# Attention backward in one kernel: E transposes moved to the end of the step, fp32 X transposes cut into eight pieces, row factors by quarters

## The chip, the cores and the metric

One core of a Trainium2 chip runs the whole kernel. The metric is the device time of one execution in microseconds. A profiled execution gives the trace: when each instruction of each engine began and ended, and the transfers. The engines are TensorE (PE; its weight loads are listed apart as PEld), VectorE (DVE), ScalarE (ACT), GpSimd (POOL) and SyncE (SP), which issues most transfers.

## What is computed

The reference is a forward pass and its gradients (a VJP) for a block of attention gated by an MLP, at S = 2048 positions, D = 512, 32 heads of 16, F = 1792:

```python
def _A_ref(x, wqkv, wo):
...
    qkv = (lambda x, *d: x.transpose(*d))((x @ wqkv).reshape(B, S, 3, H, Dh), 2, 0, 3, 1, 4)
    q, k, v = qkv[0], qkv[1], qkv[2]
    scores = jnp.einsum("bhqd,bhkd->bhqk", q, k) * (Dh ** -0.5)
    p = _softmax(scores, axis=-1)
    o = jnp.einsum("bhqk,bhkd->bhqd", p, v)
    return (lambda x, *d: x.transpose(*d))(o, 0, 2, 1, 3).reshape(B, S, D) @ wo
...
x = A_x
xn = _layernorm(x, axis=-1)
s = _A_ref(xn, A_wqkv, A_wo)
g = _silu(_B_ref(xn, B_w1, B_b1, B_w2, B_b2))
return x + s * g
...
_out, _vjp = jax.vjp(_f, A_x, A_wqkv, A_wo, B_w1, B_b1, B_w2, B_b2)
_grads = _vjp(grad_out)
```

The change is in the attention: forward and backward of softmax(QK)V for all heads, done in one pass. For each pair of heads and each 512 queries the kernel needs E = exp(scores) and G = E times (dO V^T), both as [keys, queries], and both again transposed as [queries, keys] for the gradients of K and V.

## The kernel before, in words

The kernel has three stages: `Pre` (projections, MLP forward, the gate), `attention_core`, and `Grads` (the weight gradients and dx). The order of instructions on every engine is the order in which the program emits them; there is no scheduler. A semaphore wait stands wherever a buffer or a result is needed from another engine.

`attention_core` walks over 64 blocks (16 pairs of heads, 4 chunks of 512 queries), each of 16 steps (one per 128 keys): 1024 steps, g = 0 to 1023, and 20 more to drain. In step g, PE gets in this order:

- `emit_d` and `emit_s` (L1115, L1093): d(g) for two heads, and s(g+1), the scores of the next step. All four are 32-row matmuls of 512 columns. d has three PSUM buffers (`ps_d`), s has one, which is two banks wide (`ps_s`).
- `emit_T` (L1177): seven 128x128 bf16 transposes of E(g-1) into tT, of which there is one buffer (`ps_t`). The eighth tile goes by a DMA transpose (`ekd`).
- `emit_XT` (L1233): in step 2 of a block only (`FIN_AT`), four 128x128 fp32 transposes of xs, the sums X of the block before.
- `emit_x` (L1207, L1210, L1214): twelve matmuls of 256 columns that add to X; the last four ("gts matmuls") read G(g-1). X has one buffer.
- `emit_z` (L1291): four matmuls of 512 columns that add to Z, from step g-20's point of view, with E or G transposed as the moving side and row factors W1, W2 as weights. In steps 4 to 7 and 12 to 15 of a block Z reads W2 and G (`gk`), in steps 8 to 11 and 0 to 3 W1 and E (`ek`, `ekd`). Z has one buffer. There is no Z in the first 20 steps.

ScalarE computes the exponential ets(g+1) from s(g+1) (`emit_exp`, L1102) and then copies most of tT to `ek` (`emit_cT`, L1189). DVE makes the two products gts(g) = d(g) times ets(g) (`emit_mult`, L1132, "multiplies"), and in some steps, between them, the rest of tT: `VCOPY` says how many of the seven tiles DVE takes in which of the 16 steps (nine of them have one or two). DVE also copies X to xs behind the multiplies of step 0 (L1223), XT to xt in step 2 (L1245), takes a reciprocal of its 17th columns (L1255), and after steps 3 and 11 adds Z to acc (`emit_acc`, L1303, L1305) behind the multiplies. POOL computes the row factors and the outputs from xt in ten operations per block (`emit_fin`, L1256 to L1271), behind that reciprocal, and issues the loads of the next pair of heads (`late`), each behind a small copy that waits for a multiply (L1351). SP issues the DMA transposes of gts to gk every second step (L1148), and of two tiles of ets every eighth (L1158 to L1164).

In code, the order in a step before is:

```python
emit_d(g, 0); emit_s(g + 1, 0); emit_s(g + 1, 1); emit_d(g, 1)
emit_exp(g + 1)
emit_T(g - 1); emit_XT(g)
emit_x(g - 1, "e"); emit_x(g - 1, "l"); emit_x(g - 1, "g")
emit_z(g + ZOFF)
emit_mult(g); emit_xs(g - 1); emit_fin(g)
...
emit_acc(g + ZOFF)
emit_cT(g - 1, 0, 7 - VCOPY[(g - 1) % 16], nc.scalar.copy)
emit_dmat(g)
```

Of the kernel before, what the change touches and what calls it, by code (L numbers as in the profile page):

```python
# [1028 lines left out]
def attention_core(ctx, ctx_r, tc, k, grads, Oall, dQall, dKVT_out, ident_f32, ident_bf, npairs=16, nqc=4):  # L1029
# [75 lines left out]
    def emit_d(g, hj):  # L1105
        a = a_unit(g)
        if a is None:
            return
# [6 lines left out]
        nc.tensor.matmul(d[:], lhsT=op["KVT"][r:r + 32, kb * 128:(kb + 1) * 128], rhs=op["QDT"][r:r + 32, qc * 512:(qc + 1) * 512],  # L1115
                         start=True, stop=True, tile_position=(r, 0))


    VCOPY = (0, 0, 0, 0, 1, 1, 1, 2, 1, 2, 0, 0, 1, 1, 1, 0)

    def emit_mult(g):
        a = a_unit(g)
        if a is None:
            emit_cT(g - 1, 7 - VCOPY[(g - 1) % 16], 7, nc.vector.tensor_copy)
            return
        kb = a[1]
        if kb % 2 == 0:
            cur["gts"] = gtp.tile([128, 2, 2, 512], bf16, name="gts")
        gts = cur["gts"]
        st_gt[g] = gts  # L1130
        for hj in range(2):
            nc.vector.tensor_tensor(out=gts[:, kb % 2, hj, :].rearrange("k (b q) -> k b q", b=4),  # L1132
                                    in0=st_d.pop((g, hj))[:].rearrange("k (b q) -> k b q", b=4),
                                    in1=st_et[g][:, :, hj, kb % 4, :], op=ALU.mult)
# [33 lines left out]
    def emit_T(g):  # L1168
        a = a_unit(g)
        if a is None:  # L1170
            return
        kk = a[1] % 4
        et = st_et[g]
        t = ps_t.tile([128, 7, 128], bf16, name="tT")
        for i in range(7):
# [1 line left out]
            nc.tensor.transpose(t[:, i, :], et[:, b // 2, b % 2, kk, :], ident_bf[:])  # L1177
# [5 lines left out]
    def emit_cT(g, lo, hi, copy):  # L1183

        a = a_unit(g)
        if a is None or lo == hi:
            return
        j, kb = a
        copy(out=blk[j]["Ek"][kb // 4][:, kb % 4, lo:hi].rearrange("q i k -> q (i k)").bitcast(f32),  # L1189
             in_=st_T[g][:, lo:hi].rearrange("q i k -> q (i k)").bitcast(f32))  # L1190
# [26 lines left out]
    def emit_xs(g):  # L1217
# [5 lines left out]
        nc.vector.tensor_copy(out=xs[:], in_=blk[j].pop("X")[:])  # L1223
        blk[j]["xs"] = xs

    def emit_XT(g):
        j = g // 16 - 1
        if g % 16 != FIN_AT or not 0 <= j < NB:
            return
        xs = blk[j].pop("xs")  # L1230
        XT = ps_d.tile([128, 4, 128], f32, name="XT", tag="d")
        for qb in range(4):
            nc.tensor.transpose(XT[:, qb, :], xs[:, qb * 128:(qb + 1) * 128], ident_f32[:])  # L1233
        blk[j]["XT"] = XT

    def emit_fin(g):
        j = g // 16 - 1
        if g % 16 != FIN_AT or not 0 <= j < NB:
            return
        p, qc = blocks[j]  # L1240
        NQq = k.op0["NATQq"]
        NQd = k.op0["NATQd"]
        XT = blk[j].pop("XT")
        xt = xsp.tile([128, 4, 128], f32, name="xt", tag="xs")
        nc.vector.tensor_copy(out=xt[:], in_=XT[:])  # L1245
        xf = xt[:].rearrange("q b c -> q (b c)")
        XE = xf[:, 0:256].rearrange("q (b h c) -> q b h c", b=4, h=2)
        XG = xf[:, 256:512].rearrange("q (b h c) -> q b h c", b=4, h=2)
        W1, W2 = WT[j % 2]
        st0 = qc * 4  # L1250
        nqs = NQq[:, st0:st0 + 4, :, :]
        ndo = NQd[:, st0:st0 + 4, :, :]
        bc = lambda ap: ap.to_broadcast([128, 4, 2, 16])
        rL = finp.tile([128, 4, 2, 1], f32, name="rL")
        nc.vector.reciprocal(out=rL[:], in_=XG[:, :, :, 17:18])  # L1255
        nc.gpsimd.tensor_tensor(out=W2[:, :, :, 16:32], in0=nqs, in1=bc(rL[:]), op=ALU.mult)  # L1256
        ndl = finp.tile([128, 4, 2, 1], f32, name="ndl")
        nc.gpsimd.tensor_tensor(out=ndl[:], in0=XG[:, :, :, 0:1], in1=rL[:], op=ALU.mult)
        ndr = finp.tile([128, 4, 2, 1], f32, name="ndr")
        nc.gpsimd.tensor_tensor(out=ndr[:], in0=ndl[:], in1=rL[:], op=ALU.mult)  # L1260
        nc.gpsimd.tensor_tensor(out=W1[:, :, :, 0:16], in0=ndo, in1=bc(rL[:]), op=ALU.mult)
        nc.gpsimd.tensor_tensor(out=W1[:, :, :, 16:32], in0=nqs, in1=bc(ndr[:]), op=ALU.mult)
        Ov = Oall[:, st0:st0 + 4, p * 32:(p + 1) * 32].rearrange("q b (h c) -> q b h c", h=2)
        nc.gpsimd.tensor_tensor(out=Ov, in0=XE[:, :, :, 16:32], in1=bc(rL[:]), op=ALU.mult)
        t1 = finp.tile([128, 4, 2, 16], f32, name="t1")
        nc.gpsimd.tensor_tensor(out=t1[:], in0=XE[:, :, :, 0:16], in1=bc(ndl[:]), op=ALU.mult)
        nc.gpsimd.tensor_tensor(out=t1[:], in0=XG[:, :, :, 1:17], in1=t1[:], op=ALU.add)
        rL4 = finp.tile([128, 4, 2, 1], f32, name="rL4")
        nc.gpsimd.tensor_scalar(out=rL4[:], in0=rL[:], scalar1=0.25, scalar2=None, op0=ALU.mult)
        dQv = dQall[:, st0:st0 + 4, p * 32:(p + 1) * 32].rearrange("q b (h c) -> q b h c", h=2)  # L1270
        nc.gpsimd.tensor_tensor(out=dQv, in0=t1[:], in1=bc(rL4[:]), op=ALU.mult)  # L1271

    def emit_z(g):
        u = z_unit(g)
        if u is None:
# [4 lines left out]
        Z = blk[j]["Z"]  # L1280
        for par in range(2):
            kc = 2 * kp + par
            for hj in range(2):
# [7 lines left out]
                nc.tensor.matmul(Z[r:r + 32, :], lhsT=WT[j % 2][1 - part][:, qb, hj, :], rhs=mv,  # L1291
                                 start=(part == 0 and qb == 0), stop=(part == 1 and qb == 3), tile_position=(0, r))
# [184 lines left out]
```

## Time and profile before

| what | value |
|---|---|
| time, median of 3 runs | 2214.51 us (2211.53 to 2218.92) |
| the profiled execution, its own time | 2212.67 us |
| its span, first to last instruction | 2210.8 us |
| granted TensorE clock, mean | 0.997 |
| exponentials, L1102 | 1024, 1023 ns each |
| multiplies, L1132 | 2048, 683 ns each |
| reciprocals, L1255 | 64, 204 ns each |
| copies X to xs and XT to xt | 64 each, 680 ns each |

The profile gives busy times by engine, groups of instructions (line, engine, operation, what it writes and reads, how often, the busy time, the mean duration in ns of one, and the engine's idle time before them with what ended it), and timelines: start in us from the span's start, duration in us, engine, line, and how many instructions were merged into the row. A row with x7 and 0.55 is seven instructions whose first began at the start given and whose last ended 0.55 later. The engines work on several instructions in overlap, so a duration is longer than the distance between two starts.

### The profile page before, as it was taken

What the parts mean: (1) busy time and instruction counts of PE and PEld (TensorE: products, weight loads), DVE (VectorE), ACT (ScalarE), POOL (GpSimd) and SP (SyncE); (2) the same over time, 40 slices, a digit from 0 to 9 for tenths busy, and PEclk for the clock granted to TensorE, in tenths of its full rate; (3) what the DMA queues carried; (4) which work ended last, traced back from release to release, by engine and by line L of the source; (5) the groups of instructions that cost most, each with busy time, mean ns of one, the idle gap of its engine ahead of it and who ended that gap; (6) DMA issues with size and microseconds to landing.
All of it is one profiled execution on the core that took longest, in us unless ns stands there. A gap on an engine that the chain in (4) does not pass through costs nothing.

```text
span 2210.8 us, 74213 instructions
## 1 busy us (share of the span) xinstructions
PE 2154.0 (97%) x30690; PEld 1203.2 (54%) x30690; DVE 1911.7 (86%) x3638; ACT 1734.2 (78%) x2481; POOL 590.4 (27%) x1373
## 2 busy tenths in 40 slices
PE   6999999999999999999999999999999999999998
PEld 3444555555555555555555555555555555444444
DVE  6677899999999999999999999999999998797624
ACT  4664888888888888888888888888888887784214
POOL 4375213221222222221322122222222132510002
PEclk9999999999999999999999999999999999999999
DMA  7786999999999999999999999999999999999974
GB/s 232 244 277 200 200 199 192 202 198 194 204 205 195 204 196 197 201 197 202 200 196 203 199 195 198 206 194 204 197 197 206 197 210 211 300 259 235 244 200 156
DMA packets 1422066, 461.14 MB, mean 209 GB/s; under 512 B 1334622, under 2 KB 1405918, under 8 KB 1421728
## 3 DMA queue, kind: packets, MB, share of 16 engines
q1 hardware_dynamic: 1407424, 425.46, 101.4%
q0 software_dynamic: 12720, 29.37, 5.0%
q8 instruction: 240, 3.93, 0.8%
q10 hardware_dynamic: 1584, 1.57, 0.2%
q14 instruction: 98, 0.80, 0.1%
HBM read 62.79 MB, written 64.75 MB: 58 GB/s over the span
## 4 chain that ended last, share of the span: by engine, by line
PE 89%; DVE 4%; ACT 2%; issue 2%; DMA 2%; POOL 1%; SPq 1%; ACTq 0%; DVEq 0%; POOLq 0%
PE tT L1177 24%; PE d L1115 15%; PE X L1207 10%; PE Z L1291 10%; PE X L1210 5%; PE X L1214 5%; PE s L1093 3%; PE ps_dw L742 2%; PE ps_dy L912 2%; PE ps_h L352 2%; PE ps_dw L984 2%; PE ps_m L367 2%; PE ps_dh L878 2%; PE XT L1233 1%; PE ps_qkv L210 1%
## 5 line engine op out<-in xcount | busy, mean ns | idle before, releaser
L1132 DVE TENSOR_TENSOR gts<-d,ets 128x512 bf16<-128x512 f32 x2048 | 1361.6, 683 | 99.4 <-ACT ek L1189 20.5
L1102 ACT ACTIVATE ets<-s 128x1024 bf16<-128x1024 f32 x1024 | 1047.7, 1023 | 198.6 <-PE s L1093 95.5
L1177 PE MATMUL tT<-ident_bf,ets 128*128 128x128 bf16 x7168 | 568.1, 219 | 11.7 <-ACT ek L1189 1.7
L1177 PEld LDWEIGHTS <-ets 128*128 128x128 bf16 x7168 | 444.6, 97 | 237.6 <-issue 235.5
L1189 ACT COPY ek<-tT 128x448 f32<-128x448 f32 (+2 forms) x1024 | 502.2, 490 | 2.8 <-DVE ek L1189 2.1
L1115 PE MATMUL d<-QDT,KVT 32*128 32x512 bf16 x2048 | 459.1, 385 | 0.0
L1093 PE MATMUL s<-QDT,KVT 32*128 32x512 bf16 x2048 | 401.3, 380 | 3.7 <-ACT ets L1102 3.6
L1115 PEld LDWEIGHTS <-KVT 32*128 32x128 bf16 x2048 | 145.6, 91 | 323.3 <-issue 323.3
L1207 PE MATMUL X<-ets,NAT 128*32 128x256 bf16 x4096 | 300.4, 284 | 0.3 <-DVE xs L1223 0.3
L1210 PE MATMUL X<-ets,Lc 128*32 128x256 bf16 x4096 | 289.5, 273 | 0.0
L1214 PE MATMUL X<-gts,NAT 128*17 128x256 bf16 x4096 | 289.5, 273 | 0.0
L1351 POOL COPY tick<-gts 1x2 bf16<-1x2 bf16 x205 | 35.7, 174 | 612.3 <-DVE gts L1132 612.3
L1291 PE MATMUL Z<-gk,W 128*32 128x512 bf16 x2048 | 197.9, 379 | 1.0 <-DVE acc L1305 1.0
L1291 PE MATMUL Z<-ek,W 128*32 128x512 bf16 x1792 | 198.4, 379 | 0.0
L1207 PEld LDWEIGHTS <-NAT 128*32 128x32 bf16 x4096 | 106.0, 93 | 110.8 <-issue 11.3
L1256 POOL TENSOR_TENSOR W<-NATQq,rL 128x128 bf16<-128x128 bf16 x64 | 25.4, 396 | 526.1 <-DVE rL L1255 438.4
L1093 PEld LDWEIGHTS <-KVT 32*128 32x128 bf16 x2048 | 139.2, 91 | 12.8 <-issue 9.6
L1189 DVE COPY ek<-tT 128x64 f32<-128x64 f32 (+1 forms) x576 | 131.6, 229 | 0.7
L1291 PEld LDWEIGHTS <-W 128*32 128x32 bf16 x4096 | 109.8, 97 | 11.5 <-issue 1.5
L1210 PEld LDWEIGHTS <-Lc 128*32 128x32 bf16 x4096 | 107.8, 96 | 0.0
L1214 PEld LDWEIGHTS <-NAT 128*17 128x17 bf16 x4096 | 103.4, 92 | 3.0
L1291 PE MATMUL Z<-ekd,W 128*32 128x512 bf16 x256 | 97.0, 379 | 0.0
(246 smaller groups left out, 2318.7 us busy)
## 6 DMA issues: line engine op xcount, KB each, us to landing
gk<-gts SPq DMA_TRANSPOSE x512, 5.3
H1T_s<-h1r SPq DMA_DIRECT2D x28, 256.0 KB, 4.1
HGT_s<-hgT SPq DMA_DIRECT2D x8, 896.0 KB, 4.5
DH_s<-stg SPq DMA_DIRECT2D x12, 512.0 KB, 3.2
hch<-DH_s SPq DMA_DIRECT2D x12, 512.0 KB, 4.4
gp<-H1T_s SPq DMA_DIRECT2D x9, 512.0 KB, 7.6
out_dram<-ob_w POOLq DMA_DIRECT2D x36, 128.0 KB, 4.2
NAT_s<-NS SPq DMA_DIRECT2D x4, 1056.0 KB, 6.1
```

Source lines behind the costliest of these rows:

```text
L352: nc.tensor.matmul(ps[:], lhsT=w1_sb[:, ic, fc * 128:(fc + 1) * 128], rhs=yT[:, ic, g * 512:(g + 1) * 512], start=(ic == 0), stop=(ic == I ...
L367: nc.tensor.matmul(ps[:], lhsT=hgT[:, g % 2, fc, t4 * 128:(t4 + 1) * 128], rhs=w2_sb[:, fc, :], start=(fc == 0), stop=(fc == FC - 1))
L1093: nc.tensor.matmul(s[:, hj, :], lhsT=op["KVT"][r:r + 32, kb * 128:(kb + 1) * 128], rhs=op["QDT"][r:r + 32, qc * 512:(qc + 1) * 512], start ...
L1102: nc.scalar.activation(out=st_et[g][:, :, :, a[1] % 4, :].rearrange("k b h q -> k h b q"), in_=cur["s"][:].rearrange("k h (b q) -> k h b q ...
L1115: nc.tensor.matmul(d[:], lhsT=op["KVT"][r:r + 32, kb * 128:(kb + 1) * 128], rhs=op["QDT"][r:r + 32, qc * 512:(qc + 1) * 512], start=True, ...
L1132: nc.vector.tensor_tensor(out=gts[:, kb % 2, hj, :].rearrange("k (b q) -> k b q", b=4), in0=st_d.pop((g, hj))[:].rearrange("k (b q) -> k b ...
L1177: nc.tensor.transpose(t[:, i, :], et[:, b // 2, b % 2, kk, :], ident_bf[:])
L1189: copy(out=blk[j]["Ek"][kb // 4][:, kb % 4, lo:hi].rearrange("q i k -> q (i k)").bitcast(f32), in_=st_T[g][:, lo:hi].rearrange("q i k -> q ...
L1207: nc.tensor.matmul(X[r:r + 32, 0:256], lhsT=NATt[:, kb, hj, 1:33], rhs=ev, start=(kb == 0), stop=False, skip_group_check=True, tile_positi ...
L1210: nc.tensor.matmul(X[r:r + 32, 256:512], lhsT=Lc[:], rhs=ev, start=False, stop=False, skip_group_check=True, tile_position=(0, r))
L1214: nc.tensor.matmul(X[r:r + 17, 256:512], lhsT=NATt[:, kb, hj, 0:17], rhs=gv, start=False, stop=(kb == 15), skip_group_check=True, tile_pos ...
L1291: nc.tensor.matmul(Z[r:r + 32, :], lhsT=WT[j % 2][1 - part][:, qb, hj, :], rhs=mv, start=(part == 0 and qb == 0), stop=(part == 1 and qb = ...
```

## The change

Five things change, all in `attention_core`.

- The order of a step: Z now comes right after d and s, then X, and T at the end of the step.
- The copy of tT to ek is one copy of 448 fp32 columns on ScalarE in every step; `VCOPY` and DVE's share are gone.
- The four fp32 transposes of xs in step 2 become eight, one in each of steps 1 and 3 to 9 (`XT_AT`), each of 64 rows by 128 columns. Each stands right behind the seven transposes T of its step and writes the last 64 columns of the same tT buffer, which is now a whole bank. In the next step DVE copies it out first of all (`emit_xt`), into a part of xs that has been read already, or into xt0. The last block is done at once.
- The row factors (`fin_g`: reciprocal on DVE, five POOL operations) and the outputs (`fin_e`: five POOL operations) are computed for a quarter of the block behind each such copy: four pieces have a `fin_g`, the other four a `fin_e`.
- X's copy to xs and Z's addition to acc are emitted between the two multiplies of a step rather than behind them.

```diff
-    VCOPY = (0, 0, 0, 0, 1, 1, 1, 2, 1, 2, 0, 0, 1, 1, 1, 0)
...
             if hj == 0:
-                emit_cT(g - 1, 7 - VCOPY[(g - 1) % 16], 7, nc.vector.tensor_copy)
+                emit_xs(g - 1)
+                emit_acc(g + ZOFF)
...
-        t = ps_t.tile([128, 7, 128], bf16, name="tT")
+        t = ps_t.tile([128, 512], f32, name="tT")
+        tb = t[:].bitcast(bf16).rearrange("q (i k) -> q i k", k=128)
...
-            nc.tensor.transpose(t[:, i, :], et[:, b // 2, b % 2, kk, :], ident_bf[:])
+            nc.tensor.transpose(tb[:, i, :], et[:, b // 2, b % 2, kk, :], ident_bf[:])
...
+        nc.scalar.copy(out=blk[j]["Ek"][kb // 4][:, kb % 4].rearrange("q i k -> q (i k)").bitcast(f32), in_=st_T[g][:, 0:448])
...
+    XT_AT = {1: 0, 3: 1, 4: 2, 5: 3, 6: 4, 7: 5, 8: 6, 9: 7}
+
+    def piece(g):
+        j = g // 16 - 1
+        if not 0 <= j < NB - 1 or g % 16 not in XT_AT:
+            return None
+        return j, XT_AT[g % 16]
...
+    def transpose_piece(out, j, i):
+        q0 = (256, 0)[i // 4] + 128 * (i % 4 // 2)
+        h = i % 2
+        nc.tensor.transpose(out, blk[j]["xs"][64 * h:64 * h + 64, q0:q0 + 128], ident_f32[64 * h:64 * h + 64, 64 * h:64 * h + 64])
+
     def emit_XT(g):
...
+        pc = piece(g)
+        if pc is not None:
+            transpose_piece(st_T[g - 1][:, 448:512], *pc)
...
+    def emit_xt(g):
+        pc = piece(g)
+        if pc is None:
             return
...
+        j, i = pc
+        nc.vector.tensor_copy(out=slot_of(j, i), in_=st_T[g - 1][:, 448:512])
+        (fin_g if i < 4 else fin_e)(j, i % 4, i % 4 + 1)
...
+        emit_xt(g - 1)
         emit_d(g, 0)
         emit_s(g + 1, 0)
         emit_s(g + 1, 1)
         emit_d(g, 1)
         emit_exp(g + 1)
-        emit_T(g - 1)
-        emit_XT(g)
+        emit_z(g + ZOFF)
         emit_x(g - 1, "e")
         emit_x(g - 1, "l")
         emit_x(g - 1, "g")
-        emit_z(g + ZOFF)
+        st_T.pop(g - 2, None)
+        emit_T(g - 1)
+        emit_XT(g)
         emit_mult(g)
-        emit_xs(g - 1)
-        emit_fin(g)
...
-        emit_acc(g + ZOFF)
...
-        emit_cT(g - 1, 0, 7 - VCOPY[(g - 1) % 16], nc.scalar.copy)
-        st_T.pop(g - 1, None)
+        emit_cT(g - 1)
```

More of the change, by code (lines that the diff above doesn't have):

```diff
@@ L1135, in emit_mult @@
             if hj == 0:
-                emit_cT(g - 1, 7 - VCOPY[(g - 1) % 16], 7, nc.vector.tensor_copy)
+                emit_xs(g - 1)
+                emit_acc(g + ZOFF)
     def emit_dmat(g):
@@ L1181, in emit_T, with emit_cT @@
             blk[a[0]]["Ek"][a[1] // 4] = cur["ek"]
-    def emit_cT(g, lo, hi, copy):
+    def emit_cT(g):
         a = a_unit(g)
-        if a is None or lo == hi:
+        if a is None:
             return
         j, kb = a
-        copy(out=blk[j]["Ek"][kb // 4][:, kb % 4, lo:hi].rearrange("q i k -> q (i k)").bitcast(f32),
-             in_=st_T[g][:, lo:hi].rearrange("q i k -> q (i k)").bitcast(f32))
+        nc.scalar.copy(out=blk[j]["Ek"][kb // 4][:, kb % 4].rearrange("q i k -> q (i k)").bitcast(f32), in_=st_T[g][:, 0:448])
     def emit_x(g, part):
@@ L1224, in emit_xs @@
         blk[j]["xs"] = xs
-    def emit_XT(g):
-        j = g // 16 - 1
-        if g % 16 != FIN_AT or not 0 <= j < NB:
-            return
[L1230 to L1239, printed above, removed]
-        p, qc = blocks[j]
[L1241 to L1248, printed above, removed]
-        W1, W2 = WT[j % 2]
[L1250 to L1271, printed above, removed]
@@ new lines, in attention_core, with slot_of @@
+    XT_AT = {1: 0, 3: 1, 4: 2, 5: 3, 6: 4, 7: 5, 8: 6, 9: 7}
[4 more added lines that the diff above has]
+        return j, XT_AT[g % 16]
+    def slot_of(j, i):
+        if j == NB - 1:
+            return blk[j]["xs"][:, 64 * i:64 * i + 64]
+        if i == 0:
+            return xt0[:]
+        c = (192 + 64 * i) % 512
+        return blk[j]["xs"][:, c:c + 64]
+    def transpose_piece(out, j, i):
+        q0 = (256, 0)[i // 4] + 128 * (i % 4 // 2)
+        h = i % 2
+        nc.tensor.transpose(out, blk[j]["xs"][64 * h:64 * h + 64, q0:q0 + 128], ident_f32[64 * h:64 * h + 64, 64 * h:64 * h + 64])
@@ new lines, in emit_XT @@
+    def emit_XT(g):
+        pc = piece(g)
+        if pc is not None:
+            transpose_piece(st_T[g - 1][:, 448:512], *pc)
+        elif g == NSTEP + 1:
+            j = NB - 1
+            XT = ps_d.tile([128, 512], f32, name="XT", tag="d")
+            for i in range(4):
+                q0 = (256 + 128 * i) % 512
+                nc.tensor.transpose(XT[:, 128 * i:128 * i + 128], blk[j]["xs"][:, q0:q0 + 128], ident_f32[:])
+            nc.vector.tensor_copy(out=blk[j]["xs"][:], in_=XT[:])
+            fin_g(j, 0, 4)
+            fin_e(j, 0, 4)
@@ new lines, in fin_g @@
+    def fin_g(j, b0, b1):
+        XG, tt, bs, p, bc = fin_views(j, 0, b0, b1)
+        W1, W2 = WT[j % 2]
+        nqs = k.op0["NATQq"][:, tt, :, :]
+        ndo = k.op0["NATQd"][:, tt, :, :]
+        r, nl, nr = rL[:, bs], ndl[:, bs], ndr[:, bs]
+        nc.vector.reciprocal(out=r, in_=XG[:, :, :, 17:18])
+        nc.gpsimd.tensor_tensor(out=W2[:, bs, :, 16:32], in0=nqs, in1=bc(r), op=ALU.mult)
+        nc.gpsimd.tensor_tensor(out=nl, in0=XG[:, :, :, 0:1], in1=r, op=ALU.mult)
+        nc.gpsimd.tensor_tensor(out=nr, in0=nl, in1=r, op=ALU.mult)
+        nc.gpsimd.tensor_tensor(out=W1[:, bs, :, 0:16], in0=ndo, in1=bc(r), op=ALU.mult)
+        nc.gpsimd.tensor_tensor(out=W1[:, bs, :, 16:32], in0=nqs, in1=bc(nr), op=ALU.mult)
@@ new lines, in fin_e @@
+    def fin_e(j, b0, b1):
+        XE, tt, bs, p, bc = fin_views(j, 4, b0, b1)
+        XG = fin_views(j, 0, b0, b1)[0]
+        r, nl, r4 = rL[:, bs], ndl[:, bs], rL4[:, bs]
+        Ov = Oall[:, tt, p * 32:(p + 1) * 32].rearrange("q b (h c) -> q b h c", h=2)
+        nc.gpsimd.tensor_tensor(out=Ov, in0=XE[:, :, :, 16:32], in1=bc(r), op=ALU.mult)
+        t1 = XE[:, :, :, 0:16]
+        nc.gpsimd.tensor_tensor(out=t1, in0=t1, in1=bc(nl), op=ALU.mult)
+        nc.gpsimd.tensor_tensor(out=t1, in0=XG[:, :, :, 1:17], in1=t1, op=ALU.add)
+        nc.gpsimd.tensor_scalar(out=r4, in0=r, scalar1=0.25, scalar2=None, op0=ALU.mult)
+        dQv = dQall[:, tt, p * 32:(p + 1) * 32].rearrange("q b (h c) -> q b h c", h=2)
+        nc.gpsimd.tensor_tensor(out=dQv, in0=t1, in1=bc(r4), op=ALU.mult)
@@ L1312, in emit_acc @@
                 nc.gpsimd.dma_start(out=dv[:, kp, b, :], in_=ob[b * 64:(b + 1) * 64, :])
-    FIN_AT = 2
     ZOFF = -20
+    rL, ndl, ndr, rL4 = [finp.tile([128, 4, 2, 1], f32, name=n) for n in ("rL", "ndl", "ndr", "rL4")]
+    xt0 = finp.tile([128, 64], f32, name="xt0")
+    finp.tile([128, 128], mybir.dt.uint8, name="pad_to_256f")
     late = []
```

6 lines of the change are left out of this document (added).

## The prediction

> **What bounds the kernel now.** I read the page's busy shares, then the groups of instructions, then one line's instructions for the length of a step, and last the timeline of single steps, where the waits are. The shares:
>
> ```profile
> PE 2154.0 (97%) x30690; PEld 1203.2 (54%) x30690; DVE 1911.7 (86%) x3638; ACT 1734.2 (78%) x2481; POOL 590.4 (27%) x1373
> ```
>
> PE looks like the bound, but that share is an average and counts a matmul as busy while it drains. The groups the change touches, and the multiply's line:
>
> ```profile
> L1189 ACT COPY ek<-tT 128x448 f32<-128x448 f32 (+2 forms) x1024 | 502.2, 490 | 2.8 <-DVE ek L1189 2.1 <-PE tT L1177 0.6
> L1189 DVE COPY ek<-tT 128x64 f32<-128x64 f32 (+1 forms) x576 | 131.6, 229 | 0.7
> L1233 PE MATMUL XT<-ident_f,xs 128*128 128x128 f32 x256 | 38.9, 274 | 0.0
> ```
> ```profile
> L1132 DVE TENSOR_TENSOR gts<-d,ets x2048: 649/680/694, 222.7 to 1866.7; 128x512 bf16<-128x512 f32 x187
> ```
>
> From the first to the last multiply 1644.0 us pass, 1023 steps: 1.607 us a step, 25.70 us a block of 16. One step of it, in the timeline:
>
> ```profile
> 1001.21 1.02 ACT L1102 ACTIVATE ets<-s 128x1024 bf16<-128x1024 f32 x1
> ...
> 1002.13 0.53 ACT L1189 COPY ek<-tT 128x448 f32<-128x448 f32 x1
> ...
> 1002.28 0.38 PE L1115 MATMUL d<-QDT,KVT 32*128 32x512 bf16 x1
> 1002.29 0.39 PE L1093 MATMUL s<-QDT,KVT 32*128 32x512 bf16 x2
> ...
> 1002.61 0.47 PEld L1177 LDWEIGHTS <-ets 128*128 128x128 bf16 x7 [0.23 <-issue]
> ...
> 1002.71 0.55 PE L1177 MATMUL tT<-ident_bf,ets 128*128 128x128 bf16 x7
> 1002.81 1.02 ACT L1102 ACTIVATE ets<-s 128x1024 bf16<-128x1024 f32 x1 [0.15 <-PE s L1093]
> ...
> 1003.19 0.29 PE L1207 MATMUL X<-ets,NAT 128*32 128x256 bf16 x4
> ...
> 1003.53 0.39 PE L1291 MATMUL Z<-gk,W 128*32 128x512 bf16 x4
> ...
> 1003.85 0.38 PE L1115 MATMUL d<-QDT,KVT 32*128 32x512 bf16 x1
> ...
> 1003.88 0.39 PE L1093 MATMUL s<-QDT,KVT 32*128 32x512 bf16 x2
> ...
> 1003.98 0.48 ACT L1189 COPY ek<-tT 128x384 f32<-128x384 f32 x1 [0.15 <-DVE ek L1189]
> ...
> 1004.37 1.02 ACT L1102 ACTIVATE ets<-s 128x1024 bf16<-128x1024 f32 x1
> ```
>
> The reader is to see two waits that end together. The exponential of 1001.21 ends at 1002.23, and s starts at 1002.29; that of 1002.81 ends at 1003.83, s at 1003.88: s waits for its one buffer. The copy of 1002.13 ends at 1002.66 and the transposes T start at 1002.71, though their weights were being loaded from 1002.61: T waits for its one buffer. So the floor is a ring: exponential end to s 0.05, s to exponential 0.49 (1003.88 to 1004.37), exponential 1.02: **1.56**. PE alone would take d to T's load 0.32, T to X 0.48, X to Z 0.34, Z to d 0.32: 1.46. The rest of the 1.607 is the X transposes in one step of 16 and stalls behind acc and xs. The X transposes, a step without Z, and a transpose of 14 rows behind transposes of 128 (before the attention):
>
> ```profile
> 252.42 0.55 PE L1177 MATMUL tT<-ident_bf,ets 128*128 128x128 bf16 x7
> ...
> 252.81 0.61 PE L1233 MATMUL XT<-ident_f,xs 128*128 128x128 f32 x4
> ...
> 253.35 0.29 PE L1207 MATMUL X<-ets,NAT 128*32 128x256 bf16 x4
> ...
> 254.61 0.29 PE L1207 MATMUL X<-ets,NAT 128*32 128x256 bf16 x4
> ...
> 255.06 0.39 PE L1115 MATMUL d<-QDT,KVT 32*128 32x512 bf16 x1
> ```
> ```profile
> 26.94 0.38 PE L173 MATMUL tp_ps<-ident_bf,nat 128*128 128x128 bf16 x4
> ```
> ```profile
> 27.25 0.09 PEld L279 LDWEIGHTS <-b_bf 14*128 14x128 bf16 x1
> ```
>
> **The change, part by part.** D is the start of d in a step, us.
>
> *T to the end of the step.* T no longer waits: its buffer is copied out at about D+0.7 and wanted at D+1.0. But the floor of 1.56 does not contain T. New order on PE: d to Z 0.32 (as d to T); Z to X 0.22 (512 columns, by X's 0.11 for 256 with no change of tile shape between); X to T 0.45 (254.61 to 255.06); T to d 0.48 (as T to X): 1.47, as before. The ek copy now starts after T, so a second ring appears, over two steps: s to Z 0.32, to X 0.22, to T 0.45, T to its last result 0.55, to ScalarE 0.10 (s ends 1004.27, exponential 1004.37), copy 0.53 less 0.09 (the next exponential starts 0.09 before a copy ends: 1004.46 against 1004.37), exponential 1.02, to s 0.05: 3.15, or **1.57** a step. A plain step gains nothing.
>
> *The copy wholly on ScalarE.* DVE loses 131.6 us, ScalarE's copies go to 1024 x 0.53 = 543 us, 41 more. Neither is a sum on the path: ScalarE needs 0.93 + 0.44 = 1.37 a step. The cover is the 1.57; it is gone only where DVE falls behind (below).
>
> *Eight fp32 pieces.* Removed: the four of 128 columns in step 2, 0.54 from XT to X where T to X would take 0.48 less 0.39: 0.45 a block. Added, in eight steps of 63 blocks (the last block does it at once, as before): a 64-row, 64-column transpose between T and d. How soon it follows T, no row shows. Low end 0.056, by XT behind T (of seven starts 0.39 apart); high end 0.19, by the load of 14 rows behind 128-row transposes, which starts 0.15 after the last (26.94 + 0.38 - 0.22 = 27.10 to 27.25) plus 0.04, since an fp32 load lasts 140 ns against 97. I take 0.165: every row where the tile shape changes shows 0.09 to 0.10 beyond the stream (T to X 0.15 against 0.056), and this piece changes it. The Trainium skill, "TensorEngine Tiling (Array Packing)", Key Properties, says that a change of tiling mode drains TensorE; 128 rows to 64 is one. By it the low end is out; by the XT row alone a piece would cost 0.11 less. In the built changed kernel the piece shares T's buffer, the ek copy waits for the piece too, DVE's copy of the piece waits for the ek copy, and the next T waits for that. So in a piece step: T 0.34 to its last start, 0.165, piece 0.22 (273 ns less half its 107 stream), to ScalarE 0.10, copy 0.53, to DVE 0.05, copy of 64 columns 0.21, to T 0.05: **1.665**. PE alone: 1.47 + 0.165 = 1.635; the two-step ring (3.15 + 0.165)/2 = 1.66. Three limits at once; I take 1.66, between 1.60 (0.056: (3.15 + 0.056)/2) and 1.69 (0.19).
>
> The Trainium skill's "PSUM — Partial Sum Buffer", bank collisions, says that two engines must not read one bank at once; by it this wait cannot be dropped by the program. Here the copies of 1003.73 on DVE and 1003.98 on ScalarE do run in turn.
>
> *What queues behind the piece's copy.* It stands first in DVE's queue, so both multiplies wait: copy done at about D+0.95, four times a block a reciprocal behind it (203 ns, 0.035 after the copy), then the multiplies, whose starts are 0.60 apart (two in a row take 1.27) and of which the last lasts 0.68: end D+2.4. The gts matmuls of X want it at D+1.66+0.32+0.22+0.22 = D+2.42: no stall, nothing to spare. POOL's five row-factor operations a quarter (0.2 to 0.4 us each) fit in a step of 1.66, and Z wants a quarter 0.9 us after its reciprocal. SP's transposes and POOL's loads keep their places.
>
> *acc and xs between the two multiplies, Z first.* The second multiply then ends at D+0.49+0.60+0.60+0.68 = D+2.37, X wants it at D+1.57+0.76 = D+2.33, and 0.05 passes between: 0.09 in steps 1 and 12, about 0.15 in step 4, where DVE also comes late from the first piece: 0.34 a block. Before, the like stalls were in the 25.70.
>
> *The sum.* 8 x 1.57 + 8 x 1.66 + 0.34 = 26.18 against 25.70: +0.48 a block, x 63 = **+30 us**. The profiled execution took 2212.67 (span 2210.8 and 1.9 around it), 1.8 below the median of the runs, 2214.51; on that median 2245. With 1.60: 25.70, +0 us; with 1.69: +45 us.
>
> **Rivals.**
> 1. *The piece follows T as XT did.* Piece step 1.60, no change: 2215. For: the XT row. Against: the same row has no change of tile shape, all others do.
> 2. *The piece is hidden; faster.* PE has 0.10 spare a step (1.57 less 1.47). If the piece takes no more, and its copy leaves before T wants the buffer, 16 x 1.57 + 0.34 = 25.46, -0.24 x 63 = -15: 2200. It decides below a piece step of (25.70 - 12.56 - 0.34)/8 = 1.60. For: DVE loses 131.6 us, T's wait goes. Against: the copy chain.
> 3. *DVE becomes the bound.* If xt, reciprocal and multiplies end 0.1 late in four steps and the acc step doubles its stall, +0.5 a block, +32 on the forecast: 2277. For: DVE is over 90% busy in the attention and the margin is 0.02. Against: it loses 0.13 a step in 9 steps of 16.
>
> **How the numbers follow.** Forecast 0.62 (2225 to 2262); rival 1 0.09, rival 2 0.14, rival 3 0.15. A difference under 0.3%, 6.6 us, can't be told from none here. Faster is rival 2 with a part of rival 1: 0.15; same 0.08; slower 0.77. Range 2205 to 2282: rival 1 and the upper part of 2, to rival 3 with the high end of the piece.
>
> **What would show it.** Right: steps 3 to 9 of a block 1.64 to 1.68 apart, plain ones 1.56 to 1.58; T released by DVE's piece copy in piece steps; the piece 0.15 to 0.19 behind the last T; ek copies all 128x448. Wrong: a piece 0.06 behind T, s still 0.05 behind the exponential in piece steps, or plain steps under 1.55, which would mean a ring with less in it than I see.

## The result and the profile after

The changed kernel took 2273.01 us (median of 4, 2269.70 to 2273.93) against 2215.34 for the kernel before, measured beside it (median of 4): 1.027 times as long, with a 95% interval of 1.0253 to 1.0286. The forecast was 2245, with a range to 2282: the direction and the range held, the size was half of what came. The profiled execution took 2273.3 us, span 2271.2, mean clock 0.996 (before 2212.67, 2210.8 and 0.997).

The page of the kernel after, its shares and the groups of the copies and of the pieces:

```profile
PE 2218.8 (98%) x30891; PEld 1216.8 (54%) x30942; DVE 1893.0 (83%) x3692; ACT 1796.4 (79%) x2481; POOL 914.4 (40%) x3263
...
L1189 ACT COPY ek<-tT 128x448 f32<-128x448 f32 x1024 | 545.5, 533 | 188.4 <-PE tT L1244 149.2
...
L1265 DVE COPY xs<-tT 128x64 f32<-128x64 f32 x441 | 99.2, 225 | 75.7 <-ACT ek L1189 64.9
...
L1244 PE MATMUL tT<-ident_f,xs 64*128 64x64 f32 x504 | 136.9, 272 | 0.0
```

The view of the multiply's line (minimum, median, maximum in ns; start of the first and the last):

```profile
L1131 DVE TENSOR_TENSOR gts<-d,ets x2048: 670/681/693, 222.2 to 1924.8; 128x512 bf16<-128x512 f32 x187
```

First to last multiply is now 1702.6 us against 1644.0: +58.6, which is the whole of the difference. So the loss lies inside the 1024 steps and not in the stages around them. DVE is less busy than before (83% against 86%) and the multiplies are no slower. What is new in the groups is the idle time in front of ScalarE's copy: 149.2 us of it ended with a piece (L1244), and before it was 2.8 in all.

The timeline from step 4 of a block to step 6. Rows that show one step's wait are kept:

```profile
1026.07 0.39 PE L1115 MATMUL d<-QDT,KVT 32*128 32x512 bf16 x1
...
1026.08 0.38 PE L1115 MATMUL d<-QDT,KVT 32*128 32x512 bf16 x1
...
1026.74 0.23 DVE L1265 COPY xs<-tT 128x64 f32<-128x64 f32 x1
...
1027.00 0.17 DVE L1282 RECIPROCAL rL<-xs 128x2 f32<-128x2 f32 x1
...
1027.05 0.56 PE L1178 MATMUL tT<-ident_bf,ets 128*128 128x128 bf16 x7
1027.11 1.29 DVE L1131 TENSOR_TENSOR gts<-d,ets 128x512 bf16<-128x512 f32 x2
...
1027.55 0.27 PE L1244 MATMUL tT<-ident_f,xs 64*128 64x64 f32 x1
...
1027.75 0.39 PE L1115 MATMUL d<-QDT,KVT 32*128 32x512 bf16 x1
...
1027.85 0.37 PE L1115 MATMUL d<-QDT,KVT 32*128 32x512 bf16 x1
1027.86 0.53 ACT L1189 COPY ek<-tT 128x448 f32<-128x448 f32 x1 [0.23 <-PE tT L1244]
...
1028.15 0.40 PE L1320 MATMUL Z<-gk,W 128*32 128x512 bf16 x4
...
1028.82 0.56 PE L1178 MATMUL tT<-ident_bf,ets 128*128 128x128 bf16 x7
...
1029.31 0.27 PE L1244 MATMUL tT<-ident_f,xs 64*128 64x64 f32 x1
...
1029.51 0.38 PE L1115 MATMUL d<-QDT,KVT 32*128 32x512 bf16 x1
...
1029.52 0.39 PE L1115 MATMUL d<-QDT,KVT 32*128 32x512 bf16 x1
```

Three readings. First, the piece: T begins at 1027.05, the piece at 1027.55, d at 1027.75. A step without a piece has d 0.15 behind the last T; here the piece is 0.15 behind it and d 0.20 behind the piece. Second, the second d of a step: in the steps that begin at 1026.07 and 1029.51 it follows the first by 0.01, in the one at 1027.75 by 0.10. It writes one of three buffers, the one that the first multiply of the step before must leave. That multiply started at 1027.11, behind a copy and a reciprocal (1.04 after its step's d), and 0.69 later, at about 1027.8, the buffer is free. Third, what that delays: Z follows the second d by 0.30 to 0.31 in any case, so the step that begins at 1027.75 lasts 1.76 and the one before it 1.68.

Distances between the first d matmuls of neighbouring steps, worked out from the starts in the traces, in us. The rows are medians over the blocks; the last column is the sum of the means of all 16 steps:

| kernel | 0 | 1 | 2 | 3 | 4 | 5 | 6 | 7 | 8 | 9 | 10 | 11 | 12 | 13 to 15 | block |
|---|---|---|---|---|---|---|---|---|---|---|---|---|---|---|---|
| before | 1.56 | 1.63 | 1.99 | 1.48 | 1.67 | 1.56 | 1.55 | 1.57 | 1.55 | 1.54 | 1.59 | 1.53 | 1.64 | 1.55 to 1.56 | 25.69 |
| after | 1.55 | 1.94 | 1.48 | 1.93 | 1.68 | 1.76 | 1.68 | 1.76 | 1.68 | 1.68 | 1.48 | 1.61 | 1.56 | 1.55 | 26.63 |

26.63 less 25.69 is 0.94 a block; times 63 blocks, 59 us.

### The profile page after: what moved, and what is told of

Its sections match the earlier page's. It is cut to its first block, busy times and chain, and to the rows that moved or that the text cites. A ratio compares the mean times of both kernels' runs of the same rounds, so it can differ in the third digit from the quotient of the medians.

```text
span 2271.2 us, 76421 instructions
## 1 busy us (share of the span) xinstructions
PE 2218.8 (98%) x30891; PEld 1216.8 (54%) x30942; DVE 1893.0 (83%) x3692; ACT 1796.4 (79%) x2481; POOL 914.4 (40%) x3263
## 3 DMA queue, kind: packets, MB, share of 16 engines
q10 hardware_dynamic: 1584, 1.57, 0.2%
## 4 chain that ended last, share of the span: by engine, by line
PE 87%; DVE 4%; issue 3%; ACT 2%; POOL 2%; DMA 2%; SPq 1%; ACTq 0%; DVEq 0%; POOLq 0%
PE tT L1178 21%; PE d L1115 14%; PE Z L1320 14%; PE X L1213 5%; PE X L1206 5%; PE X L1209 5%; PE tT L1244 4%; PE s L1093 2%; PE ps_dy L912 2%; PE ps_dw L984 2%; PE ps_h L352 2%; PE ps_m L367 2%; PE ps_dw L742 2%; PE ps_dh L878 2%; PE ps_dwkv L830 1%
## 5 line engine op out<-in xcount | busy, mean ns | idle before, releaser
L1131 DVE TENSOR_TENSOR gts<-d,ets 128x512 bf16<-128x512 f32 x2048 | 1308.0, 683 | 66.3 <-issue 27.1
L1189 ACT COPY ek<-tT 128x448 f32<-128x448 f32 x1024 | 545.5, 533 | 188.4 <-PE tT L1244 149.2
L1178 PEld LDWEIGHTS <-ets 128*128 128x128 bf16 x7168 | 403.6, 98 | 207.7 <-issue 192.3
L1115 PE MATMUL d<-QDT,KVT 32*128 32x512 bf16 x2048 | 471.0, 383 | 0.1
L1213 PE MATMUL X<-gts,NAT 128*17 128x256 bf16 x4096 | 303.0, 273 | 0.1
L1283 POOL TENSOR_TENSOR W<-NATQq,rL 128x32 bf16<-128x32 bf16 (+1 forms) x253 | 60.8, 240 | 546.8 <-DVE rL L1282 484.2
L1115 PEld LDWEIGHTS <-KVT 32*128 32x128 bf16 x2048 | 139.9, 90 | 87.9 <-issue 0.2
L1265 DVE COPY xs<-tT 128x64 f32<-128x64 f32 x441 | 99.2, 225 | 75.7 <-ACT ek L1189 64.9
L1093 PEld LDWEIGHTS <-KVT 32*128 32x128 bf16 x2048 | 133.8, 90 | 16.2 <-issue 8.2
L1244 PE MATMUL tT<-ident_f,xs 64*128 64x64 f32 x504 | 136.9, 272 | 0.0
L1213 PEld LDWEIGHTS <-NAT 128*17 128x17 bf16 x4096 | 117.6, 91 | 16.8 <-issue 13.5
```

The costliest lines, as they stand in the source:

```text
L1093: nc.tensor.matmul(s[:, hj, :], lhsT=op["KVT"][r:r + 32, kb * 128:(kb + 1) * 128], rhs=op["QDT"][r:r + 32, qc * 512:(qc + 1) * 512], start ...
L1178: nc.tensor.transpose(tb[:, i, :], et[:, b // 2, b % 2, kk, :], ident_bf[:])
L1189: nc.scalar.copy(out=blk[j]["Ek"][kb // 4][:, kb % 4].rearrange("q i k -> q (i k)").bitcast(f32), in_=st_T[g][:, 0:448])
L1213: nc.tensor.matmul(X[r:r + 17, 256:512], lhsT=NATt[:, kb, hj, 0:17], rhs=gv, start=False, stop=(kb == 15), skip_group_check=True, tile_pos ...
L1244: nc.tensor.transpose(out, blk[j]["xs"][64 * h:64 * h + 64, q0:q0 + 128], ident_f32[64 * h:64 * h + 64, 64 * h:64 * h + 64])
L1265: nc.vector.tensor_copy(out=slot_of(j, i), in_=st_T[g - 1][:, 448:512])
```

## Experiments

After the result two explanations stood against each other for the piece steps. The expectations call them A, the pieces' own time on PE (the transpose and the change of tile shape on both sides of it), and B, the chain of copies that a piece lengthens (T, piece, ScalarE's copy, DVE's copy, next T). Each ratio below is against the kernel before, on the same chip. The runs were made in three batches on two chips, with the kernel before at 2213.49, 2215.15 and 2214.19 us, so a difference between runs of two batches is good to about 2 us.

### The new order without the pieces (order_only)

All of the change but the pieces and the quarters: the X transposes are four of 128x128 in step 2 again, behind T, and xt, reciprocal and row factors follow as before.

Against the changed kernel:

```diff
-        emit_xt(g - 1)
...
-        pc = piece(g)
-        if pc is not None:
-            transpose_piece(st_T[g - 1][:, 448:512], *pc)
...
+        if g % 16 != FIN_AT or not 0 <= j < NB:
+            return
+        XT = ps_d.tile([128, 4, 128], f32, name="XT", tag="d")
+        for qb in range(4):
+            nc.tensor.transpose(XT[:, qb, :], xs[:, qb * 128:(qb + 1) * 128], ident_f32[:])
...
+        emit_fin(g)
```

> The new order of the step, the whole copy of tT on ScalarE, xs and acc between the multiplies, but the X transposes whole in step 2 and the row factors at once, as before. Theory A (the eight pieces cost the time: each adds 0.20 us to PE in a step that has 0.07 to 0.13 us to spare): this kernel has none, its plain steps are 1.55 as in the changed kernel (median of steps 12 to 15), step 2 has 0.45 us more, so 16 x 1.55 + 0.45 + about 0.2 of stalls behind xs and acc = 25.45 a block against 25.70: about 15 us under the kernel before, 2200 (2190 to 2212). Theory C (the order or ScalarE's longer copy costs): 2240 to 2275.

Measured 2229.60, 1.0072 (1.0055 to 1.0089): 16 us slower than before, where a gain of about 15 was expected under A and 2240 or more under C: neither came. The plain steps are 1.551, so the estimate of those was right; the 0.48 a block by which it missed 25.45 is in one place. The timeline at steps 2 to 4 of a block:

```profile
1002.83 0.61 PE L1232 MATMUL XT<-ident_f,xs 128*128 128x128 f32 x4
...
1003.47 0.69 DVE L1244 COPY xt<-XT 128x512 f32<-128x512 f32 x1 [0.27 <-PE XT L1232]
...
1004.20 0.20 DVE L1254 RECIPROCAL rL<-xt 128x8 f32<-128x8 f32 x1
1004.32 0.65 DVE L1131 TENSOR_TENSOR gts<-d,ets 128x512 bf16<-128x512 f32 x1
...
1004.88 0.68 DVE L1302 COPY acc<-Z 128x512 f32<-128x512 f32 x1
...
1005.02 0.37 PE L1115 MATMUL d<-QDT,KVT 32*128 32x512 bf16 x1
1005.48 3.23 DVE L1131 TENSOR_TENSOR gts<-d,ets 128x512 bf16<-128x512 f32 x5
1005.61 0.40 PE L1290 MATMUL Z<-gk,W 128*32 128x512 bf16 x4 [0.23 <-DVE acc L1302]
```

The copy of XT (0.69) and the reciprocal stand ahead of step 3's multiplies, the acc copy between them. So acc comes out of Z's one buffer at 1005.56, Z of step 4 waits for it until 1005.61, and behind that the last multiply of step 3 is late for X. Step 4 lasts 2.08 against the 1.55 of a plain step: 0.53 x 63 = 33 us.

### The same, with the X transposes one step earlier, and with Z two steps later (order_xt_step1, order_z22)

Both take the collision out of order_only, in two ways. The first moves the X transposes to step 1, the second shifts Z and acc by two steps.

```diff
-    FIN_AT = 2
+    FIN_AT = 1
```
```diff
-    ZOFF = -20
+    ZOFF = -22
```

> The order-only kernel with the whole X transposes in step 1 instead of step 2. Theory D (its loss of 16 us against the kernel before is the 0.53 us by which step 4 is long: XT's copy and reciprocal on DVE in step 2 push the sum of Z into acc, in step 3, so late that Z in step 4 waits 0.28 and its gts matmuls another 0.17): with XT a step earlier DVE has step 2 to catch up, step 4 falls to 1.55 to 1.6, about 0.45 x 63 = 28 us under the order-only kernel and 12 under the kernel before: 2201 (2195 to 2212). Rival (the stall only moves to steps 1 to 3): 2220 to 2235.

> The order-only kernel with Z 22 steps behind instead of 20, so that acc falls in steps 5 and 13 and not right behind XT in step 2. Theory D: step 4's 0.53 goes, and step 6 takes no new stall, since DVE has steps 3 and 4 to catch up: about 30 us under the order-only kernel: 2199 (2193 to 2210). Rival (the new order needs these stalls whatever the place): 2220 to 2235.

Measured 2217.07, 1.0008 (0.9998 to 1.0019), and 2215.34, 1.0000 (0.9988 to 1.0013). The collision went in both: step 4 falls from 2.08 to 1.65 and to 1.63. Neither gains anything over the kernel before, which both expectations had asked for. With Z shifted, the sum of a block is 25.66, and before it is 25.69. So in the three arrangements tried the order is worth nothing at best: its plain step, 1.551, is the ring of s and the exponential (0.051 from the exponential's end to s, 0.477 to the next one, 1.024 for it), 0.01 less than before. Order and copy alone are not where the 58 us come from, and not a source of a gain either.

### A piece that nothing reads (dummy64)

order_only, and behind T in steps 1 and 3 to 9 one fp32 transpose of 64 rows of the identity, into the last 64 columns of tT's bank. Nothing reads these columns; what the kernel computes is unchanged. Against order_only:

```diff
+    def emit_dummy(g):
+        if g < 16 or g >= NSTEP or g % 16 not in (1, 3, 4, 5, 6, 7, 8, 9):
+            return
+        h = g % 2
+        nc.tensor.transpose(st_T[g - 1][:, 448:512], ident_f32[64 * h:64 * h + 64, :], ident_f32[64 * h:64 * h + 64, 64 * h:64 * h + 64])
...
+        emit_dummy(g)
         emit_XT(g)
```

> The order-only kernel with eight more 64-row fp32 transposes per block (of the identity), behind T in steps 1 and 3 to 9, into the last 64 columns of tT; nobody reads them, so the ek copy waits for them but DVE does nothing for them. Extra work, the outputs stay those of the reference. Theory A: PE alone then takes 1.68 in those steps against 1.55, +0.13 x 8 x 63 = +66 us on the order-only kernel, less what step 3 absorbs: +60 (50 to 68). Theory B (the chain ek copy, DVE's piece copy, next T, and the multiplies behind that copy, is what costs): +0 to +20.

Measured 2289.98, 1.0344 (1.0329 to 1.0360): 60.4 us over order_only, as A asked; B asked for under 20. Steps 3 and 5 to 9 last 1.683, the same as steps 4, 6, 8 and 9 of the changed kernel. Step 3 in the timeline, from d to the next d:

```profile
1030.79 0.38 PE L1115 MATMUL d<-QDT,KVT 32*128 32x512 bf16 x1
...
1031.77 0.56 PE L1178 MATMUL tT<-ident_bf,ets 128*128 128x128 bf16 x7
...
1032.27 0.27 PE L1276 MATMUL tT<-ident_f 64*128 64x64 f32 x1
...
1032.47 0.39 PE L1115 MATMUL d<-QDT,KVT 32*128 32x512 bf16 x1
```

The piece costs its time with no copy behind it, and no wait stands between T, the piece and d.

### The piece is also copied (dummy64_copied)

dummy64, and DVE copies the 64 columns first of all in the next step, into bytes that nothing uses. No reciprocal follows.

```diff
+        if 16 <= g - 1 < NSTEP and (g - 1) % 16 in (1, 3, 4, 5, 6, 7, 8, 9):
+            nc.vector.tensor_copy(out=xt0, in_=st_T[g - 2][:, 448:512])
```

> As the kernel before this one, and DVE copies each dummy piece first of all in the next step, as the changed kernel does, without reciprocal or row factors (the copy goes to unused bytes). Theory A: the ring T, piece, ek copy, piece copy, T is 0.346 + 0.150 + 0.308 + 0.533 + 0.032 + 0.225 + 0.090 = 1.684, the same as PE alone, and the first multiply ends at D+1.54, under 1.68: +0 to +8 us on the kernel without the copies. Theory B: +40 or more.

Measured 2292.46, 1.0355 (1.0340 to 1.0371): 2.5 us over dummy64; the intervals of the two ratios overlap, so that is hardly told from none. The copy moves the first multiply from 0.49 to 0.81 behind its step's first d, and that alone delays nothing: in piece steps 5 to 9 the distances are 1.683 again. Step 3 is longer by 0.19 and step 4 shorter by as much: XT holds one of the three d buffers there, and the second d of step 3 waits for the last multiply of step 2. The next T starts 0.09 behind the end of the copy, and 0.05 is what T takes behind a copy that it waits for: 0.04 to spare.

### A piece of T's own shape, ahead of T (dummy128_first)

order_only, and ahead of the seven transposes one fp32 transpose of 128x128 identity, written to columns that T then writes or that nothing reads. There is no change of tile shape between it and T, and T covers it from the copy.

```diff
+        emit_dummy(g + 1)
         for i in range(7):
...
+        nc.tensor.transpose(st_T[g - 1][:, 384:512], ident_f32[:], ident_f32[:])
```

> The order-only kernel with eight more 128x128 fp32 transposes per block ahead of T in the same steps (T overwrites half of what they write; nobody reads the rest). No tile shape changes between them and T. Theory A with the change of shape as the larger part of a piece's price: a transpose adds 0.11 us (the spacing of XT's four), of which 0.07 a step is spare: +0.04 x 8 x 63 = +20 us on the order-only kernel (10 to 30). If an fp32 transpose costs the same wherever it stands and whatever its shape: +60.

Measured 2271.07, 1.0260 (1.0242 to 1.0277): 41.5 over order_only, where 10 to 30 was expected. The last four matmuls of X to the first T are 0.378 apart against 0.216 without it, so it costs PE 0.162, not the 0.11 of four such transposes in a row:

```profile
1028.43 0.28 PE L1214 MATMUL X<-gts,NAT 128*17 128x256 bf16 x4
...
1028.65 0.33 PE L1276 MATMUL tT<-ident_f 128*128 128x128 f32 x1
...
1028.81 0.55 PE L1180 MATMUL tT<-ident_bf,ets 128*128 128x128 bf16 x7
```

T's seven starts take 0.011 less behind it, so a piece step is PE's 1.482 + 0.162 - 0.011, measured 1.634. The steps' means add up to 26.60 a block against 25.93 in order_only: 0.68 x 63 = 43. Twice the rows, and still 0.04 cheaper than 64 rows behind T. Why it costs more than in a row, where its neighbours are fp32 too, no run here shows.

### A piece of the shape of d, behind T (dummy32)

dummy64 with 32 rows and 32 columns: the tile shape of d, which comes next.

```diff
+        h = g % 4
+        nc.tensor.transpose(st_T[g - 1][:, 448:480], ident_f32[32 * h:32 * h + 32, :], ident_f32[32 * h:32 * h + 32, 32 * h:32 * h + 32])
```

> The order-only kernel with eight dummy pieces as in the 64-row run, but of 32 rows by 128 columns with 32 moving columns: the tile shape of the d and s matmuls that come next, so one change of shape stands between T and d, as without a piece. Nobody reads them; the outputs stay those of the reference. If PE's change of shape and the piece's stream are the price, PE alone falls from 1.68 to about 1.53 a step. What is left is the two-step ring, because the ek copy still waits for the piece: 0.974 (s to T) + 0.346 + 0.150 + 0.308 + 0.533 - 0.104 + 1.027 + 0.058 = 3.29, 1.645 a step, +0.09 x 8 x 63 = +47 us on the order-only kernel (40 to 52), 13 under the 64-row run. Rival (the ring through ScalarE doesn't count, PE alone does): +0 to +10 on the order-only kernel.

Measured 2265.60, 1.0228 (1.0208 to 1.0248): 36 over order_only, which ran on the other chip (35 by the two ratios), between the two expectations. The timeline of two steps:

```profile
1023.03 0.56 PE L1178 MATMUL tT<-ident_bf,ets 128*128 128x128 bf16 x7
...
1023.53 0.24 PE L1276 MATMUL tT<-ident_f 32*128 32x32 f32 x1
1023.53 0.38 PE L1115 MATMUL d<-QDT,KVT 32*128 32x512 bf16 x1
...
1023.81 0.53 ACT L1189 COPY ek<-tT 128x448 f32<-128x448 f32 x1 [0.62 <-PE tT L1276]
1024.23 1.03 ACT L1102 ACTIVATE ets<-s 128x1024 bf16<-128x1024 f32 x1
...
1025.08 0.38 PE L1115 MATMUL d<-QDT,KVT 32*128 32x512 bf16 x1
1025.32 0.39 PE L1093 MATMUL s<-QDT,KVT 32*128 32x512 bf16 x2
```

On PE this piece is nearly free: d follows it by 0.005, and T to d is 0.155 against 0.152 without it. The exception is step 6, where the piece lies on rows 64 to 95, those of the first d:

```profile
1026.80 0.24 PE L1276 MATMUL tT<-ident_f 32*128 32x32 f32 x1
1026.87 0.39 PE L1093 MATMUL s<-QDT,KVT 32*128 32x512 bf16 x2
1026.88 0.38 PE L1115 MATMUL d<-QDT,KVT 32*128 32x512 bf16 x2
```

There d comes 0.081 behind it, in all blocks (0.080 to 0.085). The 64-row piece delays d by 0.204 on either half of the rows, also on rows 0 to 63, which the two d do not use (steps 4, 6 and 8 of dummy64). So sharing rows is not what the 0.204 is, and the shape is.

ScalarE's copy, though, waits for the piece's last result: in the first timeline it starts 0.43 behind the start of the last T (1023.03 + 0.35 to 1023.81), without a piece 0.257. The exponential follows the copy, and s follows the exponential: at 1025.32 it is 0.24 behind its step's d. That is the two-step ring of the prediction. By the distances of order_only's trace (s to Z 0.324, to X 0.226, to the last X 0.218, to T 0.216, to the last T 0.346, to the copy 0.257, copy 0.533, less 0.091, exponential 1.023, to s 0.051) it takes 3.103 for two steps, 1.552 each; with 0.173 more, 1.638. Steps 8 and 9 together measure 3.270, 1.635 each. In steps 1, 3 and 4 other waits hide it, so 36 us rather than the 43 that 0.086 in all eight would give. A piece that took nothing from PE would thus still have lost 36 of the 60 us that the 64-row piece costs order_only.

### The reciprocal between the multiplies (late_recip)

The changed kernel, with the reciprocal and the row factors called between the two multiplies. The copy of the piece stays in front.

```diff
-        (fin_g if i < 4 else fin_e)(j, i % 4, i % 4 + 1)
...
+                emit_fin(g - 1)
                 emit_xs(g - 1)
```

> The changed kernel with the reciprocal and the row factors moved from the front of DVE's step to the place between the two multiplies; the copy of the piece stays first. Theory A (in steps 3, 5 and 7 the second d matmul waits for a d buffer that the first multiply of the step before frees late, because the reciprocal stands ahead of it): the first multiply starts at D+0.81 instead of D+1.01 to 1.04, the wait goes from steps 5 and 7 and shrinks by 0.2 in step 3: 0.07 + 0.07 + 0.2 = 0.34 a block, 21 us under the changed kernel: 2252 (2245 to 2260), if Z in steps 5 to 7 doesn't wait for a row factor that comes 0.6 later. Rival (that wait is harmless, the step is bound by the piece on PE): 2268 to 2275.

Measured 2258.99, 1.0202 (1.0186 to 1.0219): 14 us under the kernel after, where 21 was expected; the time is within the expected range. The timeline of steps 4 and 5:

```profile
1017.99 0.38 PE L1115 MATMUL d<-QDT,KVT 32*128 32x512 bf16 x1
...
1018.65 0.22 DVE L1267 COPY xs<-tT 128x64 f32<-128x64 f32 x1
1018.80 0.68 DVE L1132 TENSOR_TENSOR gts<-d,ets 128x512 bf16<-128x512 f32 x1
...
1019.39 0.15 DVE L1289 RECIPROCAL rL<-xs 128x2 f32<-128x2 f32 x1
...
1019.67 0.39 PE L1115 MATMUL d<-QDT,KVT 32*128 32x512 bf16 x1
...
1019.68 0.38 PE L1115 MATMUL d<-QDT,KVT 32*128 32x512 bf16 x1
```

The first multiply starts at 1018.80, 0.81 behind its step's first d where after it was 1.04; its buffer is free at 1019.48, and the second d of step 5 no longer waits (1019.68). Steps 5 and 7 go from 1.757 to 1.684, step 3 from 1.931 to 1.815. So the wait of the second d is the reciprocal's doing in steps 5 and 7, and in step 3 too. There 0.13 is left over a piece step: s now starts 0.13 behind its step's first d and 0.05 behind the end of the exponential, as it must after a step as short as 1.48.

### X's copy and acc behind the multiplies (behind_mults)

The changed kernel, with the copy of X to xs and the addition to acc behind the second multiply, as in the kernel before.

```diff
-            if hj == 0:
+            if hj == 1:
                 emit_xs(g - 1)
                 emit_acc(g + ZOFF)
```

> The changed kernel with xs and acc behind the second multiply, where they were. Z now stands early in the step: after steps 3 and 11 it waits for acc, which ends 0.6 later, at D+2.4, 0.5 after Z wants its buffer; X in step 1 waits for xs by about 0.3; the waits of the gts matmuls (0.18 in step 1) go. About 1.0 - 0.3 = 0.7 more a block, +45 us on the changed kernel: 2318 (2300 to 2330). If that part of the change is what costs: 2240 or less.

Measured 2334.57, 1.0545 (1.0525 to 1.0566): 61.6 over the kernel after, where 45 was expected, and above the expected range. Step 4 of a block in the timeline:

```profile
1053.82 0.68 DVE L1332 COPY acc<-Z 128x512 f32<-128x512 f32 x1
1053.82 0.39 PE L1115 MATMUL d<-QDT,KVT 32*128 32x512 bf16 x1
...
1054.55 0.40 PE L1320 MATMUL Z<-gk,W 128*32 128x512 bf16 x4 [0.34 <-DVE acc L1332]
```

Z is now the first of the step's work behind d, and it waits 0.4 for the acc copy, in steps 4 and 12; in step 1 X waits likewise for xs. By the means, steps 1, 4 and 12 grow by 0.15, 0.35 and 0.46, and from step 5 comes 0.02 more. With Z ahead of X, the place between the multiplies is a needed part of the change: without it about as much again is lost.

## Why the prediction was right and wrong

**Right: the direction, and that a plain step gains nothing.** The forecast for it was 1.57, measured 1.551. The two runs that took the collision out of the new order stand at 1.0008 and 1.0000. T's wait for its buffer is gone, as forecast (T starts 0.205 behind the last X in steps with and without a piece), and it was not what set the time.

**Right in kind, too small: the piece step.** Forecast 1.66, measured 1.684. PE sets it, as dummy64 shows. The price of a piece on PE is 0.202 (T to d 0.354 against 0.152), where the step "I take 0.165" stands; the bounds were 0.056 and 0.19. The term looked for one change of tile shape. The trace has two in a row: T to piece 0.150 and piece to d 0.204, where T to d directly is 0.152 and pays one. The piece in d's shape (dummy32) pays for no second one and delays d by 0.005. The Trainium skill, "TensorEngine Tiling (Array Packing)", Key Properties, says that a change of tiling mode drains TensorE. The traces agree: from T to a piece of 64 or 32 rows or to d it is 0.150 to 0.152, from T to T 0.056. T's own starts are 0.056 apart, so the change from T to d takes about 0.152 - 0.056 = 0.10. PE alone without a piece is 1.482 (steps 2 and 10) where the forecast said 1.47. A piece step is then 1.482 + 0.202; against the 1.66 of the forecast, 8 x 0.024 = 0.19 a block.

**Wrong: "no stall, nothing to spare".** The step's time was good: its end at D + 2.4 puts the first multiply at about D + 1.1 (2.4 - 0.68 - 0.60), and measured it starts at D + 1.01 to 1.04 and the last one ends at D + 2.28 to 2.33. But the step asked only who waits for the last multiply, the gts matmuls, and these do not wait. The first multiply has a waiter too: it holds one of three d buffers, and PE wants that buffer for the second d of the next step, which comes ahead of Z, X and T. Step 3 is 0.25 longer than a piece step, steps 5 and 7 are 0.07 longer each: 0.39 a block, 25 us, none of it in the sum. Without the reciprocal in front, 0.13 of it stays in step 3 with s; the other 0.26 is the wait of the second d, 0.26 x 63 = 16 us, and late_recip gave 14 back. In late_recip the row factor for Z comes later too, which costs it about 1.4 us in step 5 (see POOL below).

**Wrong in size and place: acc and xs.** 0.34 a block was forecast, in steps 1, 4 and 12. All of it came in step 1: 1.935 against 1.684, 0.25. There the second multiply of step 0 ends at D + 2.52 against the forecast 2.37, since the copy of X waits for X, and the last X of step 1 waits 0.18 more; the other 0.07 is s, which waits for the exponential as in a plain step. Steps 4 and 12 show nothing (1.684, 1.555). No run took step 1's wait alone.

**Left out: POOL in 13 blocks.** The step that POOL's five row-factor operations "fit in a step of 1.66" holds except where acc of a pair of heads is complete and POOL also casts it for the output. Step 5 of such a block in the timeline of the kernel after:

```profile
361.05 0.61 POOL L1338 CAST ob<-acc 128x512 bf16<-128x512 f32 x1 [1.27 <-DVE acc L1334]
...
361.95 1.13 POOL L1341 DMA_DIRECT2D dKVT_s<-ob  x2 [0.29 <-POOL ob L1338]
...
362.59 0.39 PE L1115 MATMUL d<-QDT,KVT 32*128 32x512 bf16 x1
362.68 0.37 PE L1115 MATMUL d<-QDT,KVT 32*128 32x512 bf16 x1
363.11 0.25 POOL L1283 TENSOR_TENSOR W<-NATQq,rL 128x32 bf16<-128x32 bf16 x1
...
363.42 0.40 PE L1320 MATMUL Z<-gk,W 128*32 128x512 bf16 x4 [0.36 <-POOL W L1283]
```

The cast and the two stores stand in POOL's queue ahead of the row factor that Z reads, and Z comes 0.74 behind the second d instead of 0.30. It is 5 us in all. The traces of late_recip and behind_mults have the same wait, in 15 blocks each; no run takes it away. The rest of the irregular steps, above all 3 us in step 4, where s comes late, was not followed up.

**The forecast's sum against the measured one,** a block: 26.18 forecast, + 0.19 piece steps, - 0.15 plain steps (8 x 0.02), - 0.14 steps 2 and 10, where PE makes up what it lost (1.48), + 0.06 step 11, + 0.39 steps 3, 5 and 7 (second d, and s in step 3), - 0.09 acc and xs, + 0.18 irregular steps (the means over the medians), gives 26.62; measured 26.63.

**The rivals.** The first and second fall with the price of a piece. The third (2277) named a late DVE, and its time is the nearest to the result, but that is in part luck: its mechanism is only half there. DVE is not the bound and the gts matmuls do not wait longer in the steps with a reciprocal. It is late for one buffer.

**The chain of copies** was right as a chain and not as the limit. "T released by DVE's piece copy" does not happen, since T has 0.04 to spare, and the copy in front of the multiplies costs 2.5 us at most without a reciprocal. The Trainium skill, "PSUM — Partial Sum Buffer", bank collisions, says that two engines must not read one bank at once. The copy on DVE starts 0.03 behind the end of ScalarE's in every piece step, by a wait of the program; no run here shows what would happen without it.

**The expectation that the new order alone would gain was wrong** for a reason of the same kind as the second d: a copy and a reciprocal ahead of step 3's first multiply made acc late, and Z has one buffer. With that out of the way the 16 us went (1.0008 and 1.0000), but no gain came.

## What to carry to other kernels

An instruction that is put ahead of an engine's other work delays everyone who waits for what stands behind it: list, for each result behind it, both who reads it and whose buffer it frees, and not the last reader only. A small operation between two of other tile shapes was paid for here with a change of shape on each side; a piece in the shape of a neighbour, 128 rows ahead of T or 32 rows ahead of d, was cheaper both times (0.162 and 0.003 of PE against 0.202). When rings tie (here s with the exponential, the two-step ring through the copy, and PE alone 0.07 below them), a wait taken out of one buys nothing, and work that lengthens two of them is paid for even where one is relieved.

## What the runs showed of the hardware that was not expected

- The fp32 transposes shrink less than their size. One by itself between bf16 matmuls lasts 328 ns for 128x128 (dummy128_first), 272 for 64x64 and 243 for 32x32; four of 128x128 in a row 274 to 275 each (the groups' means).
- A 128x128 fp32 transpose between fp32 neighbours of its kind starts 0.107 after the one before; the same between bf16 matmuls and bf16 transposes of 128 rows takes 0.162 of PE.
- 64 rows behind 128 rows and ahead of 32 rows take 0.202 of PE, 32 rows there 0.003: the matmul of d on other rows starts beside the piece, 0.005 later. On the piece's own rows it starts 0.081 later.
- Matmuls of 32 rows do not start strictly in the order of the program: in step 7 of dummy32, with the piece on the rows of the first d, s starts 0.009 ahead of that d, which stands in front of it.
